# Gate transpose ahead of block 1, no dummy matmuls behind the x transposes, and the left-over rows of the last four output tiles in one 64-row stretch

## Chip, cores, metric

One core of one Trainium2 chip. The metric is the device time of one execution in microseconds (us), as a median of several runs. The span of a profile is about 1.7 us shorter than the time of the same run. All times at full precision (three decimals) are starts, ends and landings of single instructions read from the traces. In the views PE is TensorE's matmuls, PEld its weight loads, DVE VectorE, ACT ScalarE, POOL GpSimd and SP SyncE; a q behind a name marks an instruction that issues a transfer (DMA). The traces also record when the clock that PE is granted changes between half and full; "the clock rises" means that change. All runs carry the label fast, which allows 1.5% over a kernel's fastest run.

## The reference, cut to what matters

```python
# x: 2048 x 512, bf16.  Two branches, mixed by a gate
g = sigmoid((x * gate_w).sum(-1, keepdims=True))
a = A(x)    # linear attention: q, k, v, feature maps, num / den, then @ wo
b = B(x)    # z = gelu(x @ w_in); z1, z2 = halves; z2 = layernorm(z2)
            # u = z1 * (w_sp @ z2 + b_sp);  b = u @ w_out, 688 rows of w_out
return g * a + (1 - g) * b
```

The 688 rows of `w_out` are 5 blocks of 128 rows and 48 left over. The gate's dot product rides along as one more column (column 688) of the z2 weights.

## The kernel before

The head: the first two tiles of x come by plain loads and are transposed by TensorE (PE). Dummy matmuls keep PE busy until x is there.

```python
    nc.sync.dma_start(out=xs[:, 0, :], in_=x2[0:P, :])          # first x tile
    nc.scalar.dma_start(out=xs[:, 1, :], in_=x2[P:2 * P, :])    # second x tile
    load_z2w(nc.sync, 0)                                        # weights, block 0
    load_z2w(nc.scalar, 1)
    load_z2w(nc.sync, 2)
    nc.scalar.dma_start(out=gaterow[0:NDT, :], in_=...)         # gate row
    load_z2w(nc.sync, 3)
    ...
        warm_up(6)                      # dummy matmuls, 512 columns
        warm_up(1, P)
        x_T(0, 0, 1, pq_tile([P, 1, P], BF16)[:, :, :])         # transposes on PE, copies on VectorE
        x_T(0, 1, NDT, pq_tile([P, 3, P], BF16)[:, :, :])
        x_T(1, 0, 2, tp1[:, :, :])
        x_T(1, 2, NDT, pq_tile([P, 2, P], BF16)[:, :, :], on_act=True)
        warm_up(2, P)                   # two dummies of 128 columns
        one(0, 0, 0)                    # one(tile, block, half): a z matmul of 344 columns
        z_part(0, 0, HF, True)
        one(0, 1, 0)
        one(1, 0, 0)
        gate_T()                        # gate matmul, then VectorE casts it into column 688 of w_z2
        z_part(1, 0, HF, True)
        one(1, 1, 0)
        for tt in range(2):
            one(tt, 1, 1)               # 345 columns: the first that reads the gate column
```

The tail: an output tile is the sum of 4 attention matmuls (`ba_attn`), 5 of `w_out` (`ba_spat`) and one with the left-over rows (`ba_rem`). In groups of tiles the left-over matmuls are done together with 64 rows each, even tiles on rows 0 to 63, odd ones on 64 to 127. The last two tiles did theirs alone with 128 rows.

```python
    BA_GROUPS = [range(0, 4), range(4, 8), range(8, 12), range(12, 14)]

    def ba_step(tt):
        group = next(g for g in BA_GROUPS if tt in g)
        accs[tt] = acc_tile()
        ba_attn(accs[tt][:, :], tt, True, False)
        ba_spat(accs[tt][:, :], tt, False)
        if tt == group[-1]:
            for t in group:
                ba_rem(accs[t][:, :], t, halves[t % 2], True)
            ...
            for t in group:
                ba_store(accs[t][:, :], t, 0, D, False)    # ScalarE scales it, and issues the store
    ...
        ba_tile(14)                      # 5 ba_spat, 1 ba_rem of 128 rows, 4 ba_attn, store
        ba_tile(15, cuts=(0, 384, D))    # the same in two pieces of 384 and 128 columns
```

The softmax here doesn't subtract the row's maximum and nothing guards it: scores larger than these inputs give would overflow.

## Time and profile before

| | before |
|---|---|
| time, us | 207.19 median of 3 runs, 207.09 to 207.26 |
| span of the profile, us | 205.0 |
| PE busy | 201.4 us, 98% |
| PE on the chain that ended last | 98% |

From the page of before, busy times and the head of the chain that ended last:

```profile
PE 201.4 (98%) x1559; PEld 120.3 (59%) x1559; DVE 129.7 (63%) x282; ACT 75.5 (37%) x123; POOL 45.6 (22%) x76
...
PE 98%; DVE 0%; issue 0%
```

PE bounds the kernel from one end to the other. So we have to read PE's own stream, matmul by matmul. The timeline of before, PE, in the head (start, duration, line, operation, out<-in, form, count):

```profile
4.13 0.42 PE L281 MATMUL pq<-ident,xs 128*128 128x128 bf16 x2
4.34 0.42 PE L222 MATMUL zp<-const-bfloat16-1.0 128*128 128x128 bf16 x2
4.56 0.49 PE L191 MATMUL zp<-w_z,xT 128*128 128x344 bf16 x1
4.84 0.49 PE L230 MATMUL zp<-w_z,xT 128*128 128x344 bf16 x1
5.13 0.64 PE L191 MATMUL zp<-w_z,xT 128*128 128x344 bf16 x2
5.61 0.17 PE L291 MATMUL pq<-ident,gaterow 128*128 128x4 bf16 x1
```

Starts tell more than durations here. Two z matmuls start 0.287 us apart (4.56, 4.84), which is 344 columns at half clock; later ones start 0.145 us apart. The two dummies (L222) stand between the transposes and block 0. The weight loads show the wait for the gate column; timeline of before, PE's weight loads (in brackets: idle time before it):

```profile
6.07 0.10 PEld L191 LDWEIGHTS <-xT 128*128 128x128 bf16 x1 [0.19 <-issue]
```

The cast of the gate column, in the timeline of VectorE:

```profile
5.84 0.18 DVE L292 CAST w_z<-pq 128x4 bf16<-128x4 f32 x1 [1.12 <-PE pq L291]
```

It ends at 6.016 us; the weight load above and its matmul start at 6.07. The matmul before it had started at 5.779, so 5.924 was possible: 0.145 us lost.

The chain that ended last, tail of before (a piece runs from the end of the one before it; start, us, what):

```profile
197.47 0.32 PE mm L520 x2
197.79 1.18 PE mm L516 x5
198.97 0.22 PE mm L520
...
200.87 0.16 PE mm L520
...
201.96 0.06 PE mm L520
...
202.28 0.35 DVE ob L527
```

L520 is `ba_rem`. The 64-row pair costs 0.32 us, of which 0.22 is work and 0.1 the change into 64-row mode. The `ba_spat` group behind it takes 1.18 us where an ordinary one takes 1.08: the change back. Three more pieces (0.22, 0.16, 0.06) are the 128-row left-overs. Then come the stores; timeline of before, ScalarE with its DMA issues:

```profile
201.72 0.58 ACT L531 ACTIVATE ob<-mm,g_inv 128x384 bf16<-128x384 f32 x1 [0.61 <-PE mm L510]
202.33 0.34 ACTq L532 DMA_DIRECT2D out_dram<-ob  x1
```

and SyncE's queue:

```profile
202.65 0.38 SPq L529 DMA_DIRECT2D out_dram<-ob  x1
```

The 96 KB store of ScalarE lands at 203.975, the 32 KB store of SyncE at 204.154 us. What is left of the span is the program's end.

### The profile page before, as it was taken

To read this page: it belongs to the slowest core of one execution; us is meant where nothing else is said; L and a number is where in the kernel's file an instruction comes from. 1 tells how busy PE (TensorE), PEld (TensorE's weight loads), DVE (VectorE), ACT (ScalarE), POOL (GpSimd) and SP (SyncE) were. 2 spreads that over 40 slices of the span, in tenths; PEclk is the share of its full clock that TensorE was granted. 3 is DMA by queue.
4 is the path that set the end of the run, shared out by engine and by line. 5 is a ranking of instruction groups with operands and counts; after the bars stand their busy time and mean duration, and the time that the engine had idled before them with its cause. 6 is when DMAs were issued, how large, how long until landed. Compare 5 with 4: busy or idle time off the path is not lost.

```text
span 205.0 us, 3998 instructions
## 1 busy us (share of the span) xinstructions
PE 201.4 (98%) x1559; PEld 120.3 (59%) x1559; DVE 129.7 (63%) x282; ACT 75.5 (37%) x123; POOL 45.6 (22%) x76
## 2 busy tenths in 40 slices
PE   8999999999999999999999999999999999999994
PEld 4666666655665555656565666555555555665642
DVE  4477574847977687979797788555566645633330
ACT  3466678796222233332424042222351136002222
POOL 3020202021523425334242442222204220200000
PEclk9999999999999999999999999999999999999999
DMA  6999499999998017950423219763567458652842
GB/s 200 250 208 174 93 230 209 242 207 208 244 267 193 3 38 171 290 99 13 79 46 47 51 38 115 143 124 69 100 160 80 90 115 181 66 96 53 150 89 79
DMA packets 89931, 27.22 MB, mean 133 GB/s; under 512 B 84184, under 2 KB 89912, under 8 KB 89912
## 3 DMA queue, kind: packets, MB, share of 16 engines
q1 hardware_dynamic: 87312, 24.59, 63.9%
q10 hardware_dynamic: 2600, 2.37, 4.1%
q8 instruction: 12, 0.20, 0.4%
q14 instruction: 7, 0.06, 0.1%
HBM read 4.15 MB, written 2.10 MB: 30 GB/s over the span
## 4 chain that ended last, share of the span: by engine, by line
PE 98%; DVE 0%; issue 0%
PE mm L455 36%; PE zp L191 18%; PE mm L356 14%; PE mm L516 8%; PE mm L510 7%; PE mm L396 7%; PE kvacc L412 2%; PE at L468 2%; PE zp L222 1%; PE mm L520 1%; PE zp L308 0%; PE pq L281 0%; PE at L479 0%; PE zp L230 0%; PE pq L308 0%; DVE ob L527 0%
## 5 line engine op out<-in xcount | busy, mean ns | idle before, releaser
L455 PE MATMUL mm<-z2all,wspT 128*128 128x344 bf16 x512 | 79.9, 309 | 0.0
L455 PEld LDWEIGHTS <-wspT 128*128 128x128 bf16 x512 | 49.0, 98 | 25.3
L191 PE MATMUL zp<-w_z,xT 128*128 128x344 bf16 (+1 forms) x254 | 38.5, 311 | 0.0
L360 ACT ACTIVATE eq<-mm 128x512 bf16<-128x512 f32 x32 | 17.4, 594 | 51.4 <-PE mm L356 25.7
L364 DVE TENSOR_REDUCE zs<-eq 128x64 f32<-128x1024 bf16 x16 | 19.5, 1220 | 20.0 <-ACT eq L360 20.0
L191 PEld LDWEIGHTS <-xT 128*128 128x128 bf16 x254 | 24.6, 98 | 12.2 <-issue 0.2
L360 ACT ACTIVATE ek<-mm 128x512 bf16<-128x512 f32 x32 | 17.3, 600 | 27.1 <-PE mm L356 27.1
L460 DVE SCALAR_TENSOR_TENSOR ucat<-mm,bT,z1all 128x344 bf16<-128x344 f32 x32 | 17.4, 544 | 15.0 <-PE mm L455 15.0
L373 POOL TENSOR_TENSOR eq<-eq,ratio 128x512 bf16<-128x512 bf16 x16 | 16.9, 1054 | 44.6 <-DVE ratio L372 36.7
L531 ACT ACTIVATE ob<-mm,g_inv 128x512 bf16<-128x512 f32 (+1 forms) x16 | 10.9, 681 | 32.4 <-PE mm L520 26.6
L364 DVE TENSOR_REDUCE zs<-ek 128x64 f32<-128x1024 bf16 x16 | 19.3, 1209 | 2.8 <-ACT ek L360 2.8
L516 PE MATMUL mm<-wspT,uT 128*128 128x512 bf16 (+2 forms) x85 | 20.1, 367 | 0.0
L356 PEld LDWEIGHTS <-xT 128*128 128x128 bf16 x128 | 12.2, 98 | 12.0
L373 POOL TENSOR_TENSOR ek<-ek,ratio 128x512 bf16<-128x512 bf16 x16 | 16.9, 1056 | 2.2 <-DVE ratio L372 1.7
L510 PE MATMUL mm<-wspT,oT 128*128 128x512 bf16 (+2 forms) x68 | 16.6, 366 | 0.0
L356 PE MATMUL mm<-wq_p,xT 128*128 128x512 bf16 x64 | 16.4, 379 | 0.0
L396 PE MATMUL mm<-wv_sb,xT 128*128 128x512 bf16 x64 | 16.4, 379 | 0.0
L356 PE MATMUL mm<-wk_p,xT 128*128 128x512 bf16 x64 | 16.3, 379 | 0.0
L209 DVE BATCH_NORM_STATS2 bn<-z2all 128x6 f32<-128x344 bf16 x32 | 14.9, 503 | 0.0
L206 ACT ACTIVATE z2all<-zp 128x688 bf16<-128x688 f32 x16 | 11.8, 744 | 7.7 <-PE zp L191 7.7
L261 ACT ACTIVATE z1all<-zp 128x688 bf16<-128x688 f32 x16 | 11.9, 744 | 5.1 <-PE zp L191 4.6
L516 PEld LDWEIGHTS <-uT 128*128 128x128 bf16 x85 | 8.1, 98 | 9.4 <-issue 0.2
(77 smaller groups left out, 143.5 us busy)
## 6 DMA issues: line engine op xcount, KB each, us to landing
out_dram<-ob ACTq DMA_DIRECT2D x15, 128.0 KB, 2.2
wspT<-in_B_w_out_dram SPq DMA_DIRECT2D x2, 640.0 KB, 5.3
w_z<-in_B_w_in_dram SPq DMA_DIRECT2D x2, 344.0 KB, 4.7
w_z<-in_B_w_in_dram SPq DMA_DIRECT2D x3, 172.0 KB, 3.5
wv_sb<-in_A_wqkv_dram SPq DMA_DIRECT2D x2, 256.0 KB, 2.8
wspT<-in_A_wo_dram SPq DMA_DIRECT2D x2, 256.0 KB, 4.4
uT<-ucat SPq DMA_TRANSPOSE x16, 2.8
eqT<-eq SPq DMA_TRANSPOSE x16, 3.9
```

Of the source, the lines that this page charges most:

```text
L191: nc.tensor.matmul(zp[:, j, 0:n], lhsT=xT[:, dt, tt * P:(tt + 1) * P], rhs=wt[:, dt, j * HF:j * HF + n], start=(dt == 0), stop=(dt == NDT ...
L209: nc.vector.bn_stats(out=bn6[:, tt, j, :], in_=z2v[:, j, :])
L261: nc.scalar.activation(out=z1all[:, tt, :].rearrange("p (j n) -> p j n", j=2), in_=zp[:, :, 0:HF], func=AF.Gelu_apprx_tanh,)
L356: nc.tensor.matmul(ps[:, :], lhsT=xT[:, dt, tt * P:(tt + 1) * P], rhs=w[:, dt, :], start=(dt == 0), stop=(dt == NDT - 1))
L360: nc.scalar.activation(out=e[:, :, a, :], in_=ps[:, :].rearrange("p (h f) -> p h f", f=DH), func=AF.Exp, scale=1.0 - 2.0 * a)
L364: nc.vector.tensor_reduce(out=z[:].rearrange("p h a -> p (h a)"), in_=e[:].rearrange("p h a f -> p (h a) f"), axis=AX.X, op=ALU.add,)
L373: nc.gpsimd.tensor_tensor(out=e[:, :, 1, :], in0=e[:, :, 1, :], in1=ratio[:, :, None].to_broadcast([P, H, DH]), op=ALU.mult)
L396: nc.tensor.matmul(v_ps[:, :], lhsT=xT[:, dt, tt * P:(tt + 1) * P], rhs=wv_sb[:, dt, :], start=(dt == 0), stop=(dt == NDT - 1))
L455: nc.tensor.matmul(gp[:, 0:HF], lhsT=wspT[:, st, tt * P:(tt + 1) * P], rhs=z2all[:, st, j * HF:(j + 1) * HF], start=(st == 0), stop=(st == ...
L460: nc.vector.scalar_tensor_tensor(out=ucat[tt % NU][:, c0 + j * HF:c0 + (j + 1) * HF], in0=gp[:, 0:HF], scalar=bT[:, tt:tt + 1], in1=z1all[ ...
L510: nc.tensor.matmul(acc, lhsT=oTs[tt][:, g, :], rhs=wo_t[:, g, c0:c1], start=start and g == 0, stop=stop and g == NG - 1)
L516: nc.tensor.matmul(acc, lhsT=uTs[tt][:, i + ft, :], rhs=w_main[i][:, ft, c0:c1], start=start and ft == 0, stop=False)
```

## The change

Three edits. Without the dummies, block 0 should follow the transposes at once. With the gate matmul two places earlier, the gate column should be ready when it is read. With tiles 12 to 15 in one group, four left-over matmuls take two 64-row slots instead of one slot and two 128-row matmuls. The three full tiles then end together, so one is scaled on VectorE and all three are issued from SyncE's queue.

```diff
         x_T(1, 2, NDT, pq_tile([P, 2, P], BF16)[:, :, :], on_act=True)
-        warm_up(2, P)
         one(0, 0, 0)
         z_part(0, 0, HF, True)
+        gate_T()
         one(0, 1, 0)
         one(1, 0, 0)
-        gate_T()
         z_part(1, 0, HF, True)
...
-    def ba_tile(tt, cuts=(0, D)):
-        ...
+    def ba_last():
+        last = NT - 1
+        ba_step(last - 1)
+        pieces = [(acc_tile()[:, 0:384], 0, 384), (bank_tile(q_bank)[:, 0:P], 384, D)]
+        for t in BA_GROUPS[-1][:-1]:
+            ba_rem(accs[t][:, :], t)                  # tiles 12, 13, 14
+        for acc, c0, c1 in pieces:
+            ba_rem(acc, last, True, c0, c1)           # tile 15, two pieces, opens the sum
+        for n, t in enumerate(BA_GROUPS[-1][:-1]):
+            ba_store(accs[t][:, :], t, on_dve=n == 1, on_sp=True)
+        for n, (acc, c0, c1) in enumerate(pieces):
+            ba_spat(acc, last, False, c0, c1)
+            ba_attn(acc, last, False, True, c0, c1)
+            ba_store(acc, last, c0, c1, on_dve=n == 1)
...
-    BA_GROUPS = [range(0, 4), range(4, 8), range(8, 12), range(12, 14)]
+    BA_GROUPS = [range(0, 4), range(4, 8), range(8, 12), range(12, 16)]
...
-        ba_tile(14)
-        ba_tile(15, cuts=(0, 384, D))
+        ba_last()
```

More of the change, by code (lines that the diff above doesn't have):

```diff
@@ L517, in ba_spat, with ba_rem, ba_store @@
                              start=start and ft == 0, stop=False)
-    def ba_rem(acc, tt, rows, stop, c0=0, c1=D):
+    def ba_rem(acc, tt, start=False, c0=0, c1=D):
+        rows = halves[tt % 2]
         nc.tensor.matmul(
-            acc, lhsT=uTs[tt][rows, 5 * (1 - tt % 2), :], rhs=w_rem[rows, c0:c1], start=False, stop=stop)
-    def ba_store(acc, tt, c0, c1, on_dve):
+            acc, lhsT=uTs[tt][rows, 5 * (1 - tt % 2), :], rhs=w_rem[rows, c0:c1], start=start, stop=not start)
+    def ba_store(acc, tt, c0=0, c1=D, on_dve=False, on_sp=False):
         ob = work.tile([P, c1 - c0], BF16, name=f"ob{c1 - c0}", bufs=4 if c1 - c0 == D else 1)
@@ L531, in ba_store @@
             nc.scalar.activation(out=ob[:, :], in_=acc, func=AF.Copy, scale=g_inv[:, tt:tt + 1])
-            nc.scalar.dma_start(out=dst, in_=ob[:, :])
+            (nc.sync if on_sp else nc.scalar).dma_start(out=dst, in_=ob[:, :])
     def acc_tile():
@@ L536, in acc_tile @@
         return bank_tile(acc_banks[-1])
-    def ba_tile(tt, cuts=(0, D)):
-        for h, (c0, c1) in enumerate(zip(cuts, cuts[1:])):
-            acc = acc_tile()[:, 0:c1 - c0]
-            ba_spat(acc, tt, True, c0, c1)
-            ba_rem(acc, tt, slice(0, P), False, c0, c1)
-            ba_attn(acc, tt, False, True, c0, c1)
-            ba_store(acc, tt, c0, c1, h > 0)
+    def ba_last():
[12 more added lines that the diff above has]
+            ba_store(acc, last, c0, c1, on_dve=n == 1)
     def ba_step(tt):
@@ L552, in ba_step @@
             for t in group:
-                ba_rem(accs[t][:, :], t, halves[t % 2], True)
-            if tt + 2 < NT - 1:
-                attn_tile_64(tt + 2)
+                ba_rem(accs[t][:, :], t)
+            attn_tile_64(tt + 2)
             for t in group:
-                ba_store(accs[t][:, :], t, 0, D, False)
+                ba_store(accs[t][:, :], t)
     oTs = {}
```

## The prediction

> **What bounds it.** The page's first part has TensorE (PE) busy for 201.4 of 205.0 us; the chain of waits is 98% PE. In the timeline only one matmul at full clock waits for data by over 0.1 us (below); the other gaps are pairs of about 0.1 us where PE changes between 128-row and 64- or 32-row matmuls. So a nanosecond off PE's stream is one off the span, unless a load then comes late. Only the first 7 and the last 8 us change; the rest should shift.
>
> **Head.** In the timeline 344-column matmuls start 0.287 us apart at 4.6 to 5.4 us and 0.145 apart from 5.6: half clock, then full (the Trainium skill, "TensorE: Matmul & The Clock Gate", Part 1, has this warm-up; the trace agrees, with the step at about 5.5 us). I take the step to stay, as PE stays as busy.
> 1. The two dummy matmuls take 0.107 us each, at half clock. Without them block 0 starts at 4.35 instead of 4.56 us. Its inputs are there: first copy of x done at 4.07, first weights landed at 4.23, second at 4.49, next copies done at 4.52 and 4.72. No stall. The time won is half-clock time, worth half: 0.11 us.
> 2. The gate matmul comes after 2 z matmuls instead of 4. Before, its cast on VectorE ended at 6.02 us and the first reader of the gate column started at 6.07, where 5.92 was possible: 0.145 us. Now the gate matmul runs at about 4.9, the cast ends at about 5.4, the reader comes at 5.80: no wait. (The gate row's packets move at 3.83 us; its bank is free at 4.52.)
> Together about 0.26 us. Later loads have room: x for tile 2 lands at 6.73, needed at 7.3; the second z1 weights land at 9.48, needed at 10.2.
>
> **Tail.** Before: the 64-row stretch of tiles 12 and 13 took 0.42 us of PE: 0.216 the pair (starts 4 ns apart, so the halves run at once, as Part 3 of the same page says of different row groups) and 0.20 two changes of mode. The 128-row left-overs of tiles 14 and 15 took 0.216 and 0.162 + 0.056. Sum 0.85. After: one stretch of two pairs (tile 15's pieces share one half): 0.20 + 0.226 + 0.216 = 0.64. Gain 0.21 us. On the old time axis tile 15's transposed u lands at 198.65, needed at 199.3; its o at 199.73, needed at 200.7.
> The stores of 12, 13, 14 now leave at 200.5, 200.9 and 201.2 on SyncE's queue, not 1.1 us apart; ScalarE is done with them (0.69 us each) at 201.15, before the 384-column piece is ready at 201.55. The last DMA, 32 KB, leaves at 202.43 instead of 202.65 and should take the same 1.5 us. By section 3's shares 128 KB takes about 0.4 us of all 16 engines (an estimate), so I expect no queue.
>
> **Sum.** 207.19 - 0.26 - 0.21 = 206.72 us, 0.23% faster: within 2%.
>
> **Right, if:** block 0's first z matmul starts at 4.35; no wait for the gate cast; tile 2's first z matmul at 7.32 instead of 7.58; a constant shift until 195 us; the last 64-row stretch 0.64 us; the last landing 0.47 us earlier.
>
> **Wrong, if:** the clock rises later without the dummies (1 us later costs 0.5); the gate row lands after 4.9 us and PE stalls; 64-row matmuls of unequal partners run one after the other (+0.2); the bunched stores delay the last landing (up to 0.3).

## The result

| | before | after |
|---|---|---|
| time, us, median of 6 runs | 207.06 (206.90 to 207.26) | 206.43 (206.12 to 206.93) |
| ratio | 1 | 0.997, 95% interval 0.9956 to 0.9985 |
| span of the profile, us | 205.0 | 204.5 |

A ratio is the mean time of one kernel's fast runs over that of the other's of the same rounds, so it is not quite the ratio of the medians. The time is 0.29 us under the forecast of 206.72. But the single profile of after already differs from the forecast. From its page:

```profile
PE 200.8 (98%) x1557; PEld 119.9 (59%) x1557; DVE 130.4 (64%) x283; ACT 74.8 (37%) x122; POOL 45.6 (22%) x76
```

PE is again 98% of the chain that ended last.

The timeline of after, PE, in the head:

```profile
4.10 0.42 PE L280 MATMUL pq<-ident,xs 128*128 128x128 bf16 x2
4.53 0.44 PE L191 MATMUL zp<-w_z,xT 128*128 128x344 bf16 x1
4.77 0.38 PE L230 MATMUL zp<-w_z,xT 128*128 128x344 bf16 x1
4.99 0.17 PE L290 MATMUL pq<-ident,gaterow 128*128 128x4 bf16 x1
5.02 0.45 PE L191 MATMUL zp<-w_z,xT 128*128 128x344 bf16 x2
```

The dummies are gone, but block 0 starts at 4.53, hardly earlier than the 4.56 of before. PE waits 0.22 us behind the last transpose (4.208 + 0.107 = 4.315): the first weights land at 4.492 us in this run, not at 4.229. And the clock rises at 4.92 us here (the trace's record), not at 5.49: the matmul from 4.773 to 4.993 spans the rise and takes 0.22 us instead of 0.287. (The 0.24 us between 4.53 and 4.77 are not the clock: t1 below has them too, from 4.571 to 4.810, with a clock that rose at 6.53.) PE's weight loads in the timeline of after:

```profile
4.92 0.10 PEld L290 LDWEIGHTS <-gaterow 128*128 128x128 bf16 x1 [0.28 <-DMA gaterow<-in_gate_w_dram]
```

The gate row lands at 4.876, later than I had read from its packets (3.83). It costs nothing, as the z matmul ahead of the gate matmul lasts until then. The cast runs earlier, in VectorE's timeline of after:

```profile
5.23 0.18 DVE L291 CAST w_z<-pq 128x4 bf16<-128x4 f32 x1 [0.54 <-PE pq L290]
```

It ends at 5.406. The first reader of the gate column starts at 5.602, 0.145 us behind its predecessor: no wait.

The chain that ended last, tail of after:

```profile
199.07 0.54 PE mm L520 x4
199.61 0.92 PE mm L515 x5
...
201.72 0.35 DVE ob L527
```

One stretch takes 0.54 + 0.1 us (0.92 where five of 384 columns otherwise take 0.81), against 0.32 + 0.1 + 0.22 + 0.16 + 0.06 before. By starts it is 0.635 us, against 0.85. The stores, ScalarE's timeline of after:

```profile
199.42 1.27 ACT L531 ACTIVATE ob<-mm,g_inv 128x512 bf16<-128x512 f32 x2 [7.79 <-PE mm L520]
201.21 0.58 ACT L531 ACTIVATE ob<-mm,g_inv 128x384 bf16<-128x384 f32 x1 [0.52 <-PE mm L509]
201.82 0.34 ACTq L532 DMA_DIRECT2D out_dram<-ob  x1
```

and SyncE's queue:

```profile
200.14 0.37 SPq L532 DMA_DIRECT2D out_dram<-ob  x1
200.60 0.38 SPq L529 DMA_DIRECT2D out_dram<-ob  x1
201.08 0.40 SPq L532 DMA_DIRECT2D out_dram<-ob  x1
202.09 0.33 SPq L529 DMA_DIRECT2D out_dram<-ob  x1
```

ScalarE is free 0.52 us before it is needed for the 384-column piece. The last two stores land at 203.482 and 203.646.

Where do the two profiles part? PE's first 32-row matmul (the first fold of the q and k weights, about 26 us) starts 0.462 us earlier in after, not 0.26. At 40 us the lead is 0.338: a gap of 0.12 us stands between two 32-row matmuls of the second fold, at 36.5 us. It is in 2 of the 14 profiles, one of a kernel with the change's head and one of a kernel without (c1 below), and I don't know its cause. From there the lead is constant to 195 us. PE's last matmul leads by 0.559, the last landing by 0.508 us. So the sum fits the forecast (0.47), and the terms do not. The clock alone gives 0.285: it rose 0.57 us earlier, and PE does half as much work before that as after. The question is whether the change made it rise earlier.

### The profile page after: what moved, and what is told of

The parts are those of the page before. It is cut to its first block, busy times and chain, and to the rows that moved or that the text cites. A ratio compares the mean times of both kernels' runs of the same rounds, so it can differ in the third digit from the quotient of the medians.

```text
span 204.5 us, 3996 instructions
## 1 busy us (share of the span) xinstructions
PE 200.8 (98%) x1557; PEld 119.9 (59%) x1557; DVE 130.4 (64%) x283; ACT 74.8 (37%) x122; POOL 45.6 (22%) x76
## 4 chain that ended last, share of the span: by engine, by line
PE 98%; DVE 0%; issue 0%
PE mm L454 37%; PE zp L191 18%; PE mm L355 14%; PE mm L515 9%; PE mm L509 7%; PE mm L395 7%; PE kvacc L411 2%; PE at L467 2%; PE zp L222 1%; PE mm L520 1%; PE zp L307 0%; PE pq L280 0%; PE at L478 0%; PE pq L307 0%; DVE ob L527 0%; PE zp L230 0%
## 5 line engine op out<-in xcount | busy, mean ns | idle before, releaser
L531 ACT ACTIVATE ob<-mm,g_inv 128x512 bf16<-128x512 f32 (+1 forms) x15 | 10.1, 680 | 33.1 <-PE mm L520 28.5
```

## Experiments

### First call: the same kernel again, and each part alone

Theory 1: the time of the clock's rise is chance. Theory 2: taking out the dummies moves it. Each kernel ran 6 times, with 11 runs of before on the same chip.

`a1_after_again` is after, unchanged.

> The same text as the kernel after. In its first profile the full clock came at 4.92 us, against 5.49 us in the profile of before, and PE waited 0.22 us for the first weights, which landed at 4.49 us (4.23 in the profile of before). Theory 1 (chance): the time of the clock's step is drawn anew in each execution, so here it may be anywhere from 4.7 to 5.7 us, and the time moves by half of that. Theory 2 (cause): taking the dummies out makes the clock rise early, so it comes at about 4.9 us again. Both: ratio to before 0.9965 to 0.9985, block 0 starts within 0.05 us of the landing of the first weights, tail shorter by 0.22 us.

`a2_tail_alone` is after with the head of before:

```diff
         x_T(1, 2, NDT, ...)
+        warm_up(2, P)
         one(0, 0, 0)
         z_part(0, 0, HF, True)
-        gate_T()
         one(0, 1, 0)
         one(1, 0, 0)
+        gate_T()
```

> Head of before, tail of after. Both theories: the last 64-row stretch takes 0.63 to 0.65 us of PE, the tail (from the last mm matmul of the loop to the end) is 0.2 us shorter, time lower by 0.2 us (ratio 0.999). Theory 1: the clock's step may be anywhere from 4.7 to 5.7 us. Theory 2: it comes at 5.5 us, as the dummies are there.

`a3_no_dummies_alone` is before with one line taken out:

```diff
-        warm_up(2, P)
```

> Before without the two dummy matmuls. Predicted on record: 0.11 us faster. Rival: the dummies only filled time in which PE would have waited for the first weights, so block 0 starts when these land (4.2 to 4.5 us) and the gain is 0 to 0.1 us. Theory 2 (the dummies hold the clock back): step at about 4.9 us and 0.3 us more gain. The wait for the gate cast should still be there, 0.15 us or longer.

`a4_gate_alone` is before with the gate matmul moved:

```diff
         z_part(0, 0, HF, True)
+        gate_T()
         one(0, 1, 0)
         one(1, 0, 0)
-        gate_T()
```

> Before with only the gate matmul moved. Predicted on record: 0.145 us faster, no wait ahead of the first reader of the gate column. With the dummies in place the gate row (landed at 4.88 us in the profile of after) is needed at about 5.1 us, so PE does not stall for it. Theory 1: the step anywhere from 4.7 to 5.7 us. Theory 2: at about 5.5 us.

Measured:

| | median, us | range | ratio to before, 95% interval |
|---|---|---|---|
| before, 11 runs | 206.67 | 206.11 to 208.04 | |
| a1_after_again | 206.27 | 205.90 to 206.94 | 0.9984, 0.9956 to 1.0011 |
| a2_tail_alone | 206.65 | 206.11 to 206.81 | 0.9989, 0.9961 to 1.0016 |
| a3_no_dummies_alone | 206.61 | 206.30 to 207.12 | 0.9998, 0.9972 to 1.0024 |
| a4_gate_alone | 206.27 | 206.23 to 206.88 | 0.9985, 0.9960 to 1.0011 |

By time alone nothing is decided: before itself spreads over 1.9 us. The traces say more (us; the rise of a3 is worked out from the spacing of its matmuls, the others are the trace's clock records; the stall is block 0's start less the end of PE's slot before it; t1 comes further below):

| | dummies | first transpose | first weights land | block 0 starts | stall before it | clock rises | wait for the gate column |
|---|---|---|---|---|---|---|---|
| before | yes | 3.52 | 4.23 | 4.56 | 0 | 5.49 | 0.145 |
| a2 | yes | 3.46 | 4.31 | 4.53 | 0 | 6.35 | 0 |
| a4 | yes | 3.55 | 4.35 | 4.39 | 0.02 | 3.87 | 0 (gate moved) |
| after | no | 3.46 | 4.49 | 4.53 | 0.22 | 4.92 | 0 (gate moved) |
| a1 | no | 3.66 | 4.37 | 4.49 | 0 | 6.45 | 0 (gate moved) |
| a3 | no | 3.81 | 4.63 | 4.67 | 0.04 | 6.3 | 0 |
| t1 | no | 3.62 | 4.53 | 4.57 | 0.12 | 6.53 | 0 (gate moved) |

Three things follow. Theory 2 falls: the same kernel (after, a1) had its clock rise at 4.92 and at 6.45, and kernels with and without dummies had it early as well as late. Seven profiles don't exclude a small effect of the dummies on the rise. Nor was theory 1 right as I had put it: all three profiles for which I expected a rise from 4.7 to 5.7 us lay outside (6.45, 6.35, 3.87). Second, without the dummies PE is free before it can start on the first weights (0.04 us after they land) in three of four profiles, so the 0.107 us a dummy that it saves at half clock is a stall instead, in part or whole: 0.22, 0.12 and 0.04 against 0.214, and none in a1. Third, the wait for the gate column is not always there. In a2 and a3 the gate matmul stands where it stood in before, and there is no wait (a3's expectation had one), because the matmuls between it and the reader still ran at half clock and lasted longer than the cast.

An early clock has its own bound. In a4 it rose at 3.87 and PE ran into the loads; the timeline of its weight loads:

```profile
6.99 2.89 PEld L191 LDWEIGHTS <-xT 128*128 128x128 bf16 x21 [0.38 <-DMA xT<-in_A_x_dram]
10.06 0.24 PEld L191 LDWEIGHTS <-xT 128*128 128x128 bf16 x2 [0.18 <-issue]
```

The first is the wait for the third x tile, the second for the second half of the z1 weights, which landed at 10.02 us. Together PE's matmuls lost 0.32 us there.

The tail behaved in a2 as in after: the stretch took 0.636 us.

### Second call: the clock taken out of the comparison

To measure the parts without the clock's chance, VectorE holds the transposes back until about 10.8 us (I had expected about 9, and so 4 to 6 us more time; it became 6.6), when the clock has risen and all loads of the head have landed. The results stay correct. `c1_held_before`:

```diff
     nc.vector.memset(ones32[:], 1.0)
+    nc.vector.memset(z2all[:], 0.0)
+    nc.vector.memset(z1all[:, 0:8, :], 0.0)
...
-        warm_up(6)
+        warm_up(20)
```

> Before, with VectorE held back by two memsets (about 7 us) ahead of the identity that the x transposes need, and 20 first dummies instead of 6. So the transposes start at a time that VectorE sets, about 9 us, when the clock has risen and the first weights have landed. Theory 1 (the spread of the runs is the step of the clock): the spread of the runs falls from the 0.8 to 1.9 us of the free kernels to under 0.3 us. Rival (the spread comes from loads or stores): it stays at 0.6 us or more. The wait for the gate cast should be there, 0.145 us, as in the first profile of before. Time some 4 to 6 us longer than before.

`c2_held_no_dummies` is c1 without the two dummies (the edit of a3). 

> The same without the two dummies behind the transposes. If PE is free to go on, 0.11 us faster than c1_held_before (two 128-column matmuls at full clock). If the dummies only fill a wait, here for VectorE's copies of x (the third is done about 1.1 us after the first transpose), 0 to 0.03 us faster.

`c3_held_gate_early` is c1 with the edit of a4.

> The same as c1_held_before with the gate matmul moved. The gate wait is a full-clock effect: 0.13 to 0.18 us faster than c1_held_before, and no wait ahead of the first reader of the gate column. If the move only shifts a wait (PE then waits for x copies instead), 0 to 0.05 us.

The fourth kernel is on the stores. `t1_stores_on_act_queue` is after with

```diff
-            ba_store(accs[t][:, :], t, on_dve=n == 1, on_sp=True)
+            ba_store(accs[t][:, :], t)
```

> After, with the stores of tiles 12, 13 and 14 made and issued by ScalarE as in before. ScalarE then needs about 1.1 us a store (0.69 and the issue), so the 384-column piece is made 0.8 to 1.2 us later than in after, and the last landing comes 0.6 to 1.0 us later behind the last matmul (2.2 us in after). So the part of the change that moves two stores' issue and one copy off ScalarE is what lets the PE time saved in the tail be seen at all; without it time is 0.4 to 0.8 us above that of after. Rival: ScalarE has slack and nothing changes.

Measured, every run of the held kernels (granted clock, a mean over the run, in brackets):

| | us |
|---|---|
| c1 | 213.35 (1.000), 214.72 (0.992), 213.22 (0.998), 213.24 (1.000), 213.22 (1.000) |
| c2 | 213.16 (0.998), 213.12 (1.000), 214.69 (0.992), 214.57 (0.992), 214.17 (0.990), 214.66 (0.992) |
| c3 | 214.63 (0.991), 214.74 (0.992), 214.56 (0.991), 214.73 (0.991), 214.39 (0.990) |

There are two groups. Runs at a granted clock of 0.998 or more lie within 0.13 us of each other for one kernel; those at 0.992 or less are 1.0 to 1.6 us longer. All count as state fast, as that label allows 1.5%, so the verdicts over all runs mix the groups and I use only the first one. The profile of c3 fell in the second group and shows why. Its windows (stretch; length, busy PE, PEld, DVE, ACT, POOL, then granted clock, DMA share, GB/s):

```profile
11.00:12.00 1.00, 1.00 (x12) 0.71 (x10) 0.72 (x3) 0.27 (x1) 0.00 (x0) 0.56 1.04 210
12.00:14.00 2.00, 2.00 (x9) 1.06 (x8) 0.18 (x1) 0.11 (x1) 0.00 (x0) 0.50 1.20 262
14.00:15.00 1.00, 1.00 (x8) 0.63 (x7) 0.00 (x0) 0.00 (x0) 0.00 (x0) 0.74 1.25 120
```

The clock rose at 4.289, PE idled for 3.7 us (7.10 to 10.79), the clock fell at 11.116 and rose again at 14.529. These times are 6.827 and 3.413 us apart: two steps and one step of a fixed window. In the other profiles that have clock records (a3 and b1 have none) the stretches at full clock are 201.386, 197.973 or 204.8 us, which are 59, 58 and 60 such windows. So the clock changes only at the ends of a 3.413 us window whose phase is not tied to the program. The Trainium skill, "TensorE: Matmul & The Clock Gate", Part 1, section "What's actually happening", says just this: a free-running window of 4096 cycles at 1.2 GHz, 3413 ns. The traces agree to the nanosecond. The prediction cited this Part and still took the step to stay. A rise that may fall anywhere in 3.4 us moves the time by up to half of that, 1.7 us (an estimate). The runs of before spread over 1.9 us in the first call (1.1 without the slowest run) and 1.0 in each of the others. c1 bears out theory 1, with a reservation: over its four runs with a risen clock the spread is 0.13 us, but one of its five runs had the fallen clock, and over all five it is 1.5 us, not the under 0.3 that I had expected.

c1 also has the gate wait as expected. The timeline of its weight loads:

```profile
12.60 0.39 PEld L193 LDWEIGHTS <-xT 128*128 128x128 bf16 x3 [0.20 <-issue]
```

c2's expectation named two outcomes, 0.11 us, or 0 to 0.03 if the dummies only fill a wait. It was the first: its two risen runs are 0.09 us faster than those of c1 at 213.23, and block 0 starts at 11.438 instead of 11.549, with no wait for a copy. Where the inputs are there, the dummies cost their full length. c3 answered nothing about the gate, as its clock fell; it is repeated below.

t1 came out at 208.40 us, ratio 1.0074 (1.0057 to 1.0092) to before: about 2 us above after, more than the 0.4 to 0.8 expected. ScalarE's timeline of t1:

```profile
200.10 0.69 ACT L531 ACTIVATE ob<-mm,g_inv 128x512 bf16<-128x512 f32 x1 [7.79 <-PE mm L520]
...
202.70 0.69 ACT L531 ACTIVATE ob<-mm,g_inv 128x512 bf16<-128x512 f32 x1 [0.75 <-PE mm L509]
...
203.81 0.58 ACT L531 ACTIVATE ob<-mm,g_inv 128x384 bf16<-128x384 f32 x1 [0.42 <-ACT ob L531]
204.42 0.34 ACTq L532 DMA_DIRECT2D out_dram<-ob  x1
```

The stretch is the same 0.635 us, but four stores stand in a line on ScalarE: 1.1 to 1.4 us each. The 384-column piece, done by PE at 201.9, is scaled 1.9 us later. Its store lands 3.90 us behind the start of PE's last matmul, against 2.19 in after. So moving the three stores' issue and one scaling off ScalarE is no detail: without it the grouped tail loses about eight times what it wins on PE.

### Third call: gate, tail and whole change, held back, and another order of loads

28 first dummies shorten PE's idle time before the transposes. `c4_held_gate_early_28` is c3 with

```diff
-        warm_up(20)
+        warm_up(28)
```

> As c3_held_gate_early, but with 28 first dummies, so that PE idles under 3 us before the transposes and the clock should not fall back (in c3 PE idled 3.7 us and the clock fell for 3.4 us). Runs at a risen clock should lie within 0.3 us of each other. Against the risen runs of c1_held_before (213.22 to 213.35 us): 0.145 us faster if the gate wait goes and nothing takes its place, 0 to 0.05 if it is only moved.

`c5_held_tail` is a2 with the hold of c1 and 28 dummies.

> Held back, head of before, tail of after, 28 dummies. Against the risen runs of c1_held_before: 0.16 to 0.22 us faster (0.22 us of PE, less about 0.05 us that the last store takes longer in the profile of after).

`c6_held_after` is after with the same hold.

> Held back, the whole change, 28 dummies. At a clock that has risen the three parts should add: 0.11 (dummies, as c2 against c1) + 0.145 (gate) + 0.2 (tail) = 0.45 us faster than the risen runs of c1_held_before, that is 212.75 to 212.9 us. If the waits overlap (the gate matmul then waits for copies of x), 0.3 to 0.4.

`b1_weights_with_first_x` is an attempt to win the stall for the first weights:

```diff
     nc.sync.dma_start(out=xs[:, 0, :], in_=x2[0:P, :])
-    nc.scalar.dma_start(out=xs[:, 1, :], in_=x2[P:2 * P, :])
-    load_z2w(nc.sync, 0)
+    load_z2w(nc.scalar, 0)
+    nc.sync.dma_start(out=xs[:, 1, :], in_=x2[P:2 * P, :])
...
-        x_T(1, 0, 2, tp1[:, :, :])
-        x_T(1, 2, NDT, pq_tile([P, 2, P], BF16)[:, :, :], on_act=True)
         one(0, 0, 0)
         z_part(0, 0, HF, True)
+        x_T(1, 0, 2, tp1[:, :, :])
+        x_T(1, 2, NDT, pq_tile([P, 2, P], BF16)[:, :, :], on_act=True)
         gate_T()
```

> After, with the first weights loaded beside the first x tile, the second x tile behind them, and the second tile's transposes behind the first two z matmuls. In after, block 0 waits for the first weights (4.4 to 4.6 us). Here they should land at about 3.6 us and block 0 start at about 4.1 us. If nothing else then waits, the start of the first fold, less half the time of the clock's step (23.45 to 23.5 us in after), falls by 0.15 to 0.25 us. Rival: the head as a whole is bound by loads, PE then waits for the second x tile or the second weights, and it falls by less than 0.1 us. The time itself should not tell this apart from after, as the step moves it by more.

Measured at a risen clock (granted 0.998 or more), without c1's one run of 213.35, whose profile has the odd gap of 0.13 us in the second fold; the trace column is the shift of the last landing against c1, with that gap taken off c1:

| | risen runs | us | against c1 | in the trace |
|---|---|---|---|---|
| c1, before | 3 | 213.22 to 213.24 | | |
| c2, no dummies | 2 | 213.12, 213.16 | -0.09 | -0.11 |
| c4, gate early | 4 | 213.10 to 213.11 | -0.12 | -0.14 |
| c5, tail | 4 | 213.08 to 213.10 | -0.13 | -0.16 |
| c6, whole change | 4 | 212.81 to 212.84 | -0.40 | -0.41 |

c1 and c2 ran on one chip, c4 to c6 on another; that they stand so close to what the traces give is why I trust the column. (Two runs of c5 and two of c6 had the fallen clock: 214.26 to 214.59.) In c6 the weight load of the reader comes without a gap:

```profile
12.05 0.54 PEld L193 LDWEIGHTS <-xT 128*128 128x128 bf16 x4
```

So at a risen clock the three parts add, as expected, with a sum of 0.41 in the traces instead of 0.45 (by the run times, across two chips, 0.34 for the parts and 0.40 for the whole). c5 is at the lower edge of its expectation (0.16 to 0.22 us) in the trace and under it in time. On PE the sum is full: PE's last matmul leads by 0.256 (head) + 0.216 (tail) = 0.47 us. The tail's landing leads by only 0.15. The reason is in the order of the end: the 96 KB store of the 384-column piece lands last but one, and the 32 KB store 0.16 to 0.18 us behind it, in before, after, c1, c5 and c6 alike. Of the 0.216 us of PE, 0.06 is the 128-column left-over matmul (0.056), which stood behind the 384-column piece; shortening that does not bring the 96 KB store forward. That is read from the order of instructions and landings; no run took the 96 KB store away. The transfers' packets fit: in c5 those of the 32 KB store begin 0.29 us behind those of the 96 KB store (0.37 in c1) and take 0.30 us (0.27 in c1), and their end to the landing takes 0.05 us longer. The three 128 KB stores had ended 0.05 us before the 96 KB store's packets began.

b1 failed. Block 0 starts at 4.253, but the trade is bad; timeline of b1, PE:

```profile
3.65 0.61 PE L280 MATMUL pq<-ident,xs 128*128 128x128 bf16 x4
4.25 0.47 PE L191 MATMUL zp<-w_z,xT 128*128 128x344 bf16 x1
...
4.80 0.42 PE L280 MATMUL tp<-ident,xs 128*128 128x128 bf16 x2
```

PE now waits for VectorE's first copy of x (done at 4.196) where it had the second tile's transposes to do, and does these later; a z matmul then waits for their copy (done at 5.55, start at 5.607). The start of the first fold less half the time of the clock's rise is about 23.6 us (the rise, about 5.6, is an estimate from starts and durations), against 23.47 in after, 23.45 in a1 and 23.47 in t1. By the same measure the head of before had 23.65 in before but 23.47 in a2, whose clock rose late: against a2 the changed head won nothing. Time 206.57, ratio 0.9993 (0.9978 to 1.0008). No version was found that beats after.

## Why the prediction was right or wrong

The time (206.72 forecast, 206.43 measured) held, in part by luck: in the pair of profiles a clock that happened to rise early made up for a stall that the prediction had ruled out. Point by point:

- **PE bounds it, and a shift in the head is passed on to the end: right.** From the first fold to the first attention matmul it is 94.26 us in 12 of the 14 profiles, whatever the head; only the odd gap of 0.12 to 0.13 us breaks it.
- **"I take the step to stay, as PE stays as busy": wrong as a reading of one profile.** Nothing shows that the dummies move it; the rise is drawn by the phase of a window of 3.413 us. It was seen at 3.87 to 6.77 us. A single profile's clock, and with it up to 1.4 us of difference between two runs (half of these 2.9 us, an estimate), is chance. In the first pair of profiles it gave 0.285 of the 0.5 us.
- **"No stall" behind the transposes: wrong in 3 of 4 profiles.** The first weights land anywhere from 4.19 to 4.68 us, and I took the 4.23 of one profile. The term of 0.11 us is 0.107 when the weights are there (a1; 0.11 at a risen clock in c2) and nothing when they land at 4.49 (after).
- **Gate wait of 0.145 us gone: right in mechanism and size at a risen clock** (0.143 in the trace of c4, 0.12 in time). But it exists only when the clock has risen before the gate cast. In a2 and a3, with a late rise, there was no wait to remove.
- **Tail 0.21 us: right on PE (0.216 to 0.221), mis-sized in time: 0.13 to 0.16.** The failed step is "The last DMA, 32 KB, ... should take the same 1.5 us". It took 1.55. It follows the 96 KB store, which won only 0.14 to 0.15 us; that this is the reason is argued from landings and packets, not shown by a run. The bunched stores did not hold up the 96 KB store: its packets begin 0.84 us after its issue in before, after and c5 alike. That 64-row matmuls of unequal length run side by side held (starts 3 to 4 ns apart).
- **The sum of 0.47 us** is what PE saves when the clock has risen and the weights are there; 0.41 of it reaches the end. With a late clock I estimate 0.16 to 0.27 us, from 0 to 0.11 for the dummies and 0.16 for the tail. The two comparisons with before gave 0.62 and 0.35 us (differences of the means), with intervals of about 0.3 to 0.9 and -0.2 to 0.9 us; they are consistent with this and too wide to test it. Over all runs, 39 of before and 12 of this change (after and a1), the means are 206.79 and 206.42 us: 0.37 us, with a 95% interval of about 0.12 to 0.62 from their spread, several chips mixed. So the change most likely saves time; but the six runs of before in the first comparison had a mean of 207.07, the 33 others 206.74, and part of the 0.62 was luck.

Open: the gap in the second fold; and why runs of c5 and c6 still had the fallen clock when PE should have idled less than 3 us. Those runs have no profile; the last section has what c3's trace says of it.

## What to carry to other kernels

When a kernel is bound by one engine to 98%, count that engine's stream instruction by instruction; parts of 0.1 us then add up as forecast. But read the clock's phase and the landings of the first loads as ranges, not as the numbers of one profile; and to measure 0.1 us in a program whose runs spread over 1 to 2 us, hold the start back until what varies has passed. Ask of each saving at the end what the last landing really follows, and check that the engines which evacuate can take several tiles at once.

## What the Trainium skill lacked or had wrong

- "TensorE: Matmul & The Clock Gate", Part 1: the page puts the transition at about 4 us of sustained activity, plus or minus 0.5 us. With PE busy from 0.84 us the records here have it from 3.87 to 6.77 us, 3.0 to 5.9 us behind the first matmul. So the spread seen is 2.9 us, most of a window, and the rise can come less than one window (3.41 us) after the start. The same part says that the ramp costs under 1% of a typical kernel. That agrees (in before PE's own work ran at half clock from 3.52 to 5.49 us, so I estimate a cost of 1.0 us in 207), but it is about twice what this change saves.
- The same part gives one idle window as what lowers the clock. In c3 less than that was enough. Counting windows from its clock records, the one that ended with the fall ran from 7.70 to 11.116 us; PE idled until 10.79 and then did transposes, so at most 3.09 of the 3.41 us were idle (unless transposes do not count as activity, which no run tests). In c2 PE idled 2.9 us, but a window's end at 9.27 split that into 1.4 and 1.5, and the clock stayed. Runs of c5 and c6 had a lower granted clock (0.991 to 0.992) although, by an estimate from their matmul counts and c3's times, PE idled only 2.0 to 2.2 us even with a rise as early as 4.29 or 3.87. How little idle time is enough was not measured.
- "TensorEngine Tiling (Array Packing)", section "Tiling Modes", Key Properties: the page says that a change of tiling mode drains TensorE and gives no figure. Here it is 0.095 us into a 64-row stretch and 0.09 to 0.10 us out of it, the same at each stretch that goes straight back to 128 rows, and about as much for 32 rows (0.096 into it; out of it 0.11 from the last start to the next, the last matmul included). So a stretch costs 0.2 us and must save more to pay.
- "TensorE: Matmul & The Clock Gate", Part 3: that row groups run at once (starts 3 to 4 ns apart) agrees. The page does not say that it holds for matmuls of unequal length; here it does, with 512 columns beside 384 and then 128.
